# First-layer blocks taken four at a time, with two 64-row remainders side by side in the array

## The chip, the cores and the metric

The kernel runs on one core of one Trainium2 chip, in one launch. The metric is the device time of the whole launch in microseconds; of the kernel before there are three runs, of which the median counts. A profiled execution of its own gives the durations of single instructions.

## What is computed

The input x (8 x 3584 x 192) goes through a causal depthwise filter of 7 taps, whose weights are a softmax per head of 24 channels. The result, 28672 tokens of 192 channels, goes through a layer of 8 experts with a capacity of 3584 tokens each:

```python
out = einsum('hk,bskhg->bshg', softmax(weight), x_unfolded)     # 28672 x 192
logits = out @ w_gate                                           # 28672 x 8
# (token, expert) pairs in falling order of logit; a token goes to the first expert with room
for e in range(8):
    h = maximum(x[assigned == e] @ w1[e], 0)                    # 192 -> 1024
    y[assigned == e] = h @ w2[e]                                # 1024 -> 192
```

All is in 32-bit floats. The kernel splits each factor of the two products into a high part of type float32r and a low part (the rest), and adds three of the four partial products.

## The kernel before, in words

Up to about 164 us of the profile the filter runs as matmuls with a Toeplitz matrix (tile `cv`), with the logits (`pl`) between them; the assignment of tokens to experts is worked out in small steps among all that follows. From then on the class `FFN` works through 56 tiles of 512 tokens of one expert each. What follows is about this second part, and above all about its last 18 tiles (three each of the experts 2 to 7), which start at about 900 us.

`run` (L1455) is a hand-written order. Its outer loop goes over the tiles i, its inner loop over eight stages f. A stage issues, in this order:

- `l1` (L1330): block f of the first layer of tile i, that is 128 of the 1024 hidden rows for 512 tokens. It is five matmuls of 512 columns into one PSUM bank `ph` (pool of 3): (ah, xh), (al, xh), (ah, xl), (dh, xd), (dl, xd). Here ah and al are the high and low parts of the first 128 rows of w1, dh and dl those of the other 64; xa holds the first 128 channels of the tokens, high in xa[:, 0] and low in xa[:, 1]. The array has 128 rows, the remainder 64: xd holds the high part in its rows 0 to 63 and the low part in rows 64 to 127, dh stands twice, and dl (tile `dl`, `DL`) has zeros in rows 64 to 127, which `wpool` puts there once (L1186). Then ScalarE writes hh, the relu of the bank, and VectorE writes hl, the relu less hh.
- `prep` (L1441): a step of the preparation of tile i + 1. In the last tiles that is `shuffle` (L1384): steps 0 to 4 are 16 transposes of 32 x 32 blocks on VectorE (4, 3, 3, 3, 3) from the gathered rows `xg` into `xs`; in step 5 ScalarE writes the high parts xa[:, 0] and xd[0:64]; in step 6 VectorE writes the low parts xa[:, 1] and xd[64:128].
- `l2` (L1349): a quarter of a 128-token block's second layer, for the tile before: four pairs of matmuls (384 and 192 columns) into a bank `y` (pool of 2), with hh and hl of tile i - 1 as the stationary factor. After each odd stage `store` takes the block out: ScalarE writes `yt`, VectorE adds it into `yo`, and GpSimd later scatters `yo` to the output.
- `wsplit` (L1239): weights of a later tile. For the last 18 tiles all parts of w1 were kept in DRAM earlier, and a piece "W1" loads them with two DMAs on SyncE's queue (L1255, L1256), three tiles ahead of their use.

Each engine works through its own instructions in the order of issue. The queue of TensorE holds what `l1` and `l2` issue and, once the assignment is done, nothing else; so in the last 18 tiles the order above is all that sets what stands behind what.

Every matmul, activation and vector instruction of this part is issued through a helper and so has line L56 in the profile; the tile names tell them apart.

Of the kernel before, what the change touches and what calls it, by code (L numbers as in the profile page):

```python
# [6 lines left out]
F32 = mybir.dt.float32  # L7
BF = mybir.dt.bfloat16
I32 = mybir.dt.int32
FR = mybir.dt.float32r  # L10
AF = mybir.ActivationFunctionType
OP = mybir.AluOpType
# [1148 lines left out]
class FFN:  # L1161
# [3 lines left out]
    def __init__(self, tc, nc, attn, w1, w2, out, ident, wr, drm):  # L1165
        self.tc, self.nc = tc, nc

        self.kept1 = [drm.tile([128, 3, F], F32, name="kw%d" % e) for e in range(NE)]
        self.keptd = [drm.tile([64, F], F32, name="kd%d" % e) for e in range(NE)]
        self.scr = [drm.tile([6, 32, 4, 128], F32, name="scr%d" % j) for j in range(2)]  # L1170
        self.kept2 = [drm.tile([128, 8, 2 * D], F32, name="kv%d" % e) for e in range(NE)]
        self.attn, self.w1, self.w2, self.out, self.ident, self.wr = attn, w1, w2, out, ident, wr
        self.bg = lambda: None
        self.busy = lambda: False
        self.WT, self.RAW, self.XG, self.XT, self.H, self.Y, self.XS = {}, {}, {}, {}, {}, {}, {}
        self.wpa, self.wpb, self.DL = [None, None], [None, None], [None, None]
        self.scat, self.late = [], []
        self.free = set()
        self.xg = None


# [57 lines left out]
    def wsplit(self, i, eng):  # L1239

        self.turns += 1
        while self.owed and self.owed[0] <= self.turns:
            self.owed.pop(0)
            self.wload()
        if self.done == len(self.pieces) or self.pieces[self.done][0] > i:
            return
        V, A = self.nc.vector, self.nc.scalar
        _, ky, j, what, q, keep = self.pieces[self.done]
        wp = self.wpa[j]
        e = ky[0]  # L1250
        if what == "W1" or (what, q) == ("a", 0):
            W = wp.tile([128, 3, F], FR, name="w1")
            self.WT[ky] = [W[:, 0], W[:, 1], W[:, 2], self.DL[j]]
        if what == "W1":
            self.nc.sync.dma_start(W.bitcast(F32), self.kept1[e])  # L1255
            self.nc.sync.dma_start(self.DL[j][0:64].bitcast(F32), self.keptd[e])  # L1256
            self.done += 1
            return
        if what == "W2":
            t = self.wpb[j].tile([128, 8, 2 * D], FR, name="w2")  # L1260
            self.WT[ky].append(t)
            self.nc.sync.dma_start(t.bitcast(F32), self.kept2[e])
            self.done += 1
            return
        r = self.RAW.pop(self.done)
        if (what, q) == ("w", 0):
            self.WT[ky].append(self.wpb[j].tile([128, 8, 2 * D], FR, name="w2"))
        t = self.WT[ky]
        if what == "w":
            r = r[:, 0:2 * D].rearrange("p (k d) -> p k d", d=D)  # L1270
            s = slice(2 * q, 2 * q + 2)
            hi, lo = t[4][:, s, 0:D], t[4][:, s, D:2 * D]
        else:
            s = slice(512 * q, 512 * q + 512)
            hi, lo = (t[0][:, s], t[1][:, s]) if what == "a" else (t[2][:, s], t[3][0:64, s])
        A.activation(hi, r, AF.Copy)
        n = 64 if what == "d" else 128
        eng.tensor_tensor(lo, r[0:n], hi[0:n].bitcast(F32), op=OP.subtract)
        S = self.nc.sync
        if not keep:  # L1280
            pass
        elif what == "w":
            S.dma_start(self.kept2[e][:, s], t[4][:, s].bitcast(F32))
        elif what == "a":
            S.dma_start(self.kept1[e][:, 0, s], hi.bitcast(F32))
            S.dma_start(self.kept1[e][:, 1, s], lo.bitcast(F32))
        else:
            S.dma_start(self.kept1[e][:, 2, s], hi.bitcast(F32))
            S.dma_start(self.keptd[e][:, s], lo.bitcast(F32))
        self.done += 1  # L1290
        if ky[1] < NE:
            self.wload()
        else:
            self.owed.append(self.turns + 1)
# [35 lines left out]
    def l1(self, i, key, f):  # L1330
# [15 lines left out]
        nc.dve = max(nc.dve, nc.act)  # L1346
        nc.vector.scalar_tensor_tensor(hl[:, f], p, 0.0, hh[:, f].bitcast(F32), op0=OP.max, op1=OP.subtract)

    def l2(self, i, key, b, half):  # L1349
        nc = self.nc  # L1350
        hh, hl = self.H[i]
        w = self.wt(key)[4]
        if half == 0:
            self.Y[i, b] = self.py.tile([128, 512], F32, name="y")
        y = self.Y[i, b]
        s = slice(128 * b, 128 * b + 128)
        for k in range(4 * half, 4 * half + 4):
            nc.tensor.matmul(y[:, 0:2 * D], hh[:, k, s], w[:, k], start=(k == 0), stop=False, skip_group_check=True)
            nc.tensor.matmul(y[:, 0:D], hl[:, k, s], w[:, k, 0:D], start=False, stop=(k == 7), skip_group_check=True)
            if k % 4 == 1:  # L1360
                self.bg()
# [22 lines left out]
    def shuffle(self, i, step):  # L1384

        V, A = self.nc.vector, self.nc.scalar
        if step == 0:
            self.XS[i] = self.xp.tile([128, 2, 4, 128], F32, name="xs")
            self.XT[i] = (self.xs.tile([128, 2, 512], FR, name="xa"), self.xs.tile([128, 512], FR, name="xd"))
            self.todo = [(q, c) for q in range(4) for c in range(4)]  # L1390
        t = self.XS[i]
        xa, xd = self.XT[i]
        if step < 5:
            for q, c in self.todo[:4 if step == 0 else 3]:

                n = 2 if c < 2 else 1
                s = slice(32 * q, 32 * q + 32)
                x = self.XG[i][s]
                src = x[:, :, 32 * c:32 * c + 32][:, None] if n == 1 else bass.AP(
                    tensor=x.tensor, offset=x.offset + 32 * c, ap=[x.ap[0], [128, 2], [D, 4], [1, 32]])  # L1400
                V.transpose(t[32 * c:32 * c + 32, 0:n, :, s], src)
            del self.todo[:4 if step == 0 else 3]
        a, d = t[:, 0].rearrange("p b t -> p (b t)"), t[0:64, 1].rearrange("p b t -> p (b t)")
        if step == 5:
            self.XG.pop(i)
            A.activation(xa[:, 0], a, AF.Copy)
            A.activation(xd[0:64], d, AF.Copy)
        elif step == 6:
            V.tensor_tensor(xa[:, 1], a, xa[:, 0].bitcast(F32), op=OP.subtract)
            V.tensor_tensor(xd[64:128], d, xd[0:64].bitcast(F32), op=OP.subtract)  # L1410
            self.XS.pop(i)
# [43 lines left out]
    def run(self, idx_of, at, eng, free):  # L1455


        tiles = self.tiles
        n = len(tiles)
        for i in range(n + 1):  # L1460
            at(i)
            for f in range(8):
                if i + 2 < n and f == (4 if tiles[i + 2][1][1] == 4 and tiles[i + 1][1][1] < 4 else 0):
                    self.gather(i + 2, idx_of(tiles[i + 2], True), NTOK if tiles[i + 2][1][1] else NTOK // 2)
                if i < n:
                    self.l1(i, tiles[i][0], f)
                self.bg()
                if i + 2 < n and f == 6 and free() and not self.swapped(i + 2):
                    self.free.add(i + 2)
                if i + 1 < n:  # L1470
                    self.prep(i + 1, f)
                if i + 2 < n and f == 6 and self.swapped(i + 2):
                    self.turn(i + 2, -1)
                if i:
                    self.l2(i - 1, tiles[i - 1][0], f // 2, f % 2)
                    if f % 2:
                        self.store(i - 1, f // 2, idx_of(tiles[i - 1])[f // 2])
                        if f == 7:
                            self.H.pop(i - 1)
                self.bg()  # L1480
                if i < n:
                    self.wsplit(i, eng(f))
                if not f % 2 or i == n and f == 7:
                    self.scatter()
# [9 lines left out]
def moe_kernel(ctx, tc, x, weight, wg, w1, w2, out):  # L1494
    nc = Pace(tc.nc)
# [5 lines left out]
    with ExitStack() as cw:  # L1501
# [4 lines left out]
        oh = pool(cw, "ohp", 5)  # L1506
# [3 lines left out]
        r = Route(tc, nc, LT, lst, wk, drm)  # L1510
        r.oh_pool = oh
        r.bg = lambda: bgp.tile([128, 512], F32, name="bg")
        ff = FFN(tc, nc, attn, w1, w2, out, r.ident, wr, drm)
# [11 lines left out]
        tiles, n = [], 0  # L1525
# [42 lines left out]
        bg = Steps(nc, r, (half(0), tail(), half(1), rest()))  # L1568
# [150 lines left out]
                bg.drain(2)  # L1719

        ff.free = set()
        ff.run(idx_of, at, lambda f: V, lambda: not bg.gens)
    bi = lst.tile([128, 1], I32, name="bi")
    nc.vector.tensor_copy(bi, r.bad)
# [32 lines left out]
```

## Time and profile before

| | |
|---|---|
| three runs: lowest, median, highest | 1235.33, 1237.59, 1238.16 us |
| profiled execution: time, span of its instructions | 1247.95 us, 1246.2 us |
| mean granted TensorE clock | 0.993 |
| TensorE busy | 1208.1 us, 97% |
| VectorE busy | 983.6 us, 79% |
| ScalarE busy | 560.8 us, 45% |
| GpSimd busy | 535.4 us, 43% |

In rows of the profile, PE is TensorE, PEld its loads of stationary factors, DVE VectorE, ACT ScalarE, POOL GpSimd, SPq SyncE's queue. A row "A us, B" of the timeline gives the start in us from the span's start and the length; instructions of one kind in a row are put together with their count, and idle time of the engine ahead of them stands in brackets with what ended it. Matmuls are pipelined: a matmul's length includes its way through the array, so that two in a row overlap, and what one costs is the distance from its start to the next one's.

### The profile page before, as it was taken

How to read it: one execution, taken by the hardware profiler on the slowest of the kernel's cores; microseconds unless marked ns; L12 is line 12 of the kernel's file. 1: busy time of each engine (PE TensorE's matmuls, PEld its weight loads, DVE VectorE, ACT ScalarE, POOL GpSimd, SP SyncE). 2: the span in 40 equal slices, each digit the busy share in tenths (PEclk: the TensorE clock that was granted, in tenths of full speed). 3: DMA queues.
4: the chain of work that ended last, by engine and by line, in shares of the span. 5: the costliest groups of instructions: out<-in, count | busy, mean ns of one | idle time of the engine just before them, and what ended most of it. 6: DMA issues, size and time to landing. Idle time of an engine off the chain costs nothing.

```text
span 1246.2 us, 21782 instructions
## 1 busy us (share of the span) xinstructions
PE 1208.1 (97%) x7694; PEld 1036.6 (83%) x7694; DVE 983.6 (79%) x2122; ACT 560.8 (45%) x1251; POOL 535.4 (43%) x524
## 2 busy tenths in 40 slices
PE   5999899999999999999999999999999999999997
PEld 2445578889989898889888889999999999999997
DVE  7388778988898988889889866777777777777772
ACT  4454455556435554445544443333333333343332
POOL 3000233535455554555465445445434544444522
PEclk9999999999999999999999999999999999999999
DMA  9999664569526473746343442114233222413100
GB/s 242 332 338 321 216 220 123 147 156 305 170 85 176 156 229 110 246 132 216 102 132 98 128 106 73 38 46 158 72 118 107 96 98 96 158 58 136 48 23 28
DMA packets 129220, 182.02 MB, mean 146 GB/s; under 512 B 21632, under 2 KB 91728, under 8 KB 127440
## 3 DMA queue, kind: packets, MB, share of 16 engines
q1 hardware_dynamic: 86496, 104.15, 27.5%
q0 software_dynamic: 21504, 44.07, 11.9%
q10 hardware_dynamic: 21104, 32.34, 7.9%
q8 instruction: 62, 1.02, 0.3%
q14 instruction: 54, 0.44, 0.1%
HBM read 102.38 MB, written 78.12 MB: 145 GB/s over the span
## 4 chain that ended last, share of the span: by engine, by line
PE 83%; DVE 6%; DMA 5%; issue 2%; ACT 1%; SPq 1%; another core or an unknown queue 0%; POOL 0%; POOLq 0%; ACTq 0%; DVEq 0%
PE ph L56 39%; PE y L56 38%; DMA X<-in_x_dram 4%; PE cv L56 2%; PE bg L56 2%; DVE X L56 1%; DVE aT L56 1%; DMA attn<-a 1%; DVE hl L56 1%; PE pl L56 1%; DMA raw<-in_moe_w_dram 1%; PE px L56 0%; DVE yo L56 0%; SPq L569 0%
## 5 line engine op out<-in xcount | busy, mean ns | idle before, releaser
L56 PE MATMUL y<-w,hh 128*128 128x384 f32 x1792 | 535.6, 355 | 0.0
L56 ACT ACTIVATE hh<-ph 128x512 fp32r<-128x512 f32 x448 | 267.7, 598 | 451.1 <-PE ph L56 389.6
L56 PE MATMUL y<-w,hl 128*128 128x192 f32 x1792 | 448.9, 251 | 0.0
L56 DVE SCALAR_TENSOR_TENSOR hl<-ph,hh 128x512 fp32r<-128x512 f32 x448 | 307.8, 687 | 128.7 <-ACT hh L56 101.4
L56 PE MATMUL ph<-xa,w 128*128 128x512 f32 x1344 | 395.2, 402 | 0.2 <-DVE hl L56 0.2
L56 PEld LDWEIGHTS y<-w,hl 128*128 128x128 f32 x1792 | 340.9, 190 | 16.2
L56 PEld LDWEIGHTS y<-w,hh 128*128 128x128 f32 x1792 | 336.3, 188 | 20.9 <-issue 2.9
L1377 POOL DMA_INDIRECT out_dram<-yo,ia x128 | 145.3, 1135 | 236.8 <-DVE yo L56 194.0
L56 PEld LDWEIGHTS ph<-xa,w 128*128 128x128 f32 x1344 | 218.4, 189 | 21.4 <-issue 1.6
L1377 POOL DMA_INDIRECT out_dram<-yo,ib x96 | 95.2, 991 | 220.5 <-DVE yo L56 213.1
L56 PE MATMUL ph<-xd,w 128*128 128x512 f32 x448 | 177.4, 396 | 0.0
L1302 POOL DMA_INDIRECT xg<-attn,ja x128 | 141.3, 1104 | 80.8 <-issue 39.2
L56 PE MATMUL ph<-xd,dl 128*128 128x512 f32 x448 | 174.2, 389 | 0.2 <-issue 0.2
L56 DVE STREAM_TRANSPOSE xs<-xg 32x128 f32<-32x128 f32 (+2 forms) x408 | 164.8, 404 | 6.6
L56 ACT ACTIVATE yt<-y 128x192 f32<-128x192 f32 x224 | 73.1, 326 | 111.5 <-PE y L56 71.8
L56 PE MATMUL cv<-X,TH 118*128 118x384 f32 x256 | 104.5, 536 | 17.7 <-DVE TH L56 11.4
L56 DVE TENSOR_TENSOR yo<-y,yt 128x192 f32<-128x192 f32 x224 | 79.2, 354 | 49.6 <-ACT yt L56 46.0
L1302 POOL DMA_INDIRECT xg<-attn,jb x96 | 103.6, 1079 | 29.3 <-issue 29.3
L56 PEld LDWEIGHTS ph<-xd,dl 128*128 128x128 f32 x448 | 84.2, 188 | 20.2 <-issue 0.5
L56 PEld LDWEIGHTS ph<-xd,w 128*128 128x128 f32 x448 | 84.0, 187 | 19.7 <-issue 0.6
L56 PEld LDWEIGHTS cv<-X,TH 118*128 118x128 f32 x256 | 46.7, 203 | 50.0 <-issue 15.0
L56 ACT ACTIVATE a<-cv 128x384 f32<-128x384 f32 x128 | 59.7, 492 | 50.0 <-PE cv L56 26.9
(237 smaller groups left out, 920.2 us busy)
## 6 DMA issues: line engine op xcount, KB each, us to landing
attn<-a ACTq DMA_DIRECT2D x16, 1344.0 KB
X<-in_x_dram SPq DMA_DIRECT2D x17, 672.0 KB
raw<-in_moe_w_dram SPq DMA_DIRECT2D x56, 192.0 KB
X<-in_x_dram ACTq DMA_DIRECT2D x15, 672.0 KB
kw<-w SPq DMA_DIRECT2D x36, 256.0 KB
kv<-w SPq DMA_DIRECT2D x24, 384.0 KB
scr<-xs SPq DMA_DIRECT2D x96, 96.0 KB
w<-kw SPq DMA_DIRECT2D x6, 1536.0 KB
```

The costliest lines, as they stand in the source:

```text
L56: return f(*a, **k)
L1302: self.nc.gpsimd.indirect_dma_start(out=t[:, b], out_offset=None, in_=self.attn[0:rows], in_offset=bass.IndirectOffsetOnAxis(ap=idx[b], ax ...
L1377: st = self.nc.gpsimd.indirect_dma_start(out=self.out, out_offset=bass.IndirectOffsetOnAxis(ap=idx, axis=0), in_=o, in_offset=None, bounds ...
```

## The change

It concerns the tiles whose w1 was loaded by a "W1" piece, the last 18. Three things are different there.

First, `l1x4` takes the place of `l1`. In stages 0 and 4 it does four blocks at once; in the other stages of such a tile there is no first-layer work. Of its four banks one is of the pool `bg` (2 banks, idle by then), three are the `ph` banks. It issues the first four matmuls of each of the four blocks, then the four matmuls with dl, then the four pairs of hh and hl. `prep`, `l2`, `store` and the rest stay at their stages.

Second, the four matmuls with dl have 64 rows each. Those of even blocks use rows 0 to 63 of `dl` and of xd, those of odd blocks rows 64 to 127 of `dl` and of a new tile xe, so that neighbours stand in different halves of the array's rows and write to different banks.

Third, for this dl is loaded from DRAM twice, into both halves, and step 5 of `shuffle` writes the high part of the 64 channels a second time on ScalarE, into xe[64:128] (a buffer named `oa`).

```diff
+        self.both = set()
+        self.XE = {}
...
-            self.nc.sync.dma_start(self.DL[j][0:64].bitcast(F32), self.keptd[e])
+            for q in range(2):
+                self.nc.sync.dma_start(self.DL[j][64 * q:64 * q + 64].bitcast(F32), self.keptd[e])
+            self.both.add(ky)
...
+    def l1x4(self, i, key, f0):
+
+        nc = self.nc
+        if f0 == 0:
+            self.H[i] = (self.hp[i % 2].tile([128, 8, 512], FR, name="hh"),
+                         self.hp[i % 2].tile([128, 8, 512], FR, name="hl"))
+        hh, hl = self.H[i]
+        ah, al, dh, dl = self.wt(key)[0:4]
+        xa, xd = self.XT[i]
+        xe = self.XE[i]
+        ps = [self.more("bg") if f == f0 else self.ph.tile([128, 512], F32, name="ph") for f in range(f0, f0 + 4)]
+        for f, p in zip(range(f0, f0 + 4), ps):
+            s = slice(128 * f, 128 * f + 128)
+            for n, (wt, xx) in enumerate(((ah, xa[:, 0]), (al, xa[:, 0]), (ah, xa[:, 1]), (dh, xd))):
+                nc.tensor.matmul(p, wt[:, s], xx, start=(n == 0), stop=False)
+        for f, p in zip(range(f0, f0 + 4), ps):
+            s, r = slice(128 * f, 128 * f + 128), slice(64 * (f % 2), 64 * (f % 2) + 64)
+            nc.tensor.matmul(p, dl[r, s], (xe if f % 2 else xd)[r], start=False, stop=True)
+        for f, p in zip(range(f0, f0 + 4), ps):
+            nc.scalar.activation(hh[:, f], p, AF.Relu)
+            nc.dve = max(nc.dve, nc.act)
+            nc.vector.scalar_tensor_tensor(hl[:, f], p, 0.0, hh[:, f].bitcast(F32), op0=OP.max, op1=OP.subtract)
...
             A.activation(xd[0:64], d, AF.Copy)
+            if self.tiles[i][0] in self.both:
+                self.XE[i] = self.more("xe")
+                A.activation(self.XE[i][64:128], d, AF.Copy)
...
-                if i < n:
+                if i in self.XE:
+                    if f % 4 == 0:
+                        self.l1x4(i, tiles[i][0], f)
+                elif i < n:
                     self.l1(i, tiles[i][0], f)
...
+        ff.more = lambda name: r.bg() if name == 'bg' else oh.tile([128, 512], FR, name='oa')
```

What this moves is seen best in the second half of a tile, stages 4 to 7. On VectorE, before, from the hl of stage 4 to the end of the tile (`xs<-xg` are transposes of step 4, `xa<-xs,xa` and `xd<-xs,xd` the low parts of step 6):

```order
L56 SCALAR_TENSOR_TENSOR hl<-ph,hh 128x512
L56 STREAM_TRANSPOSE xs<-xg 32x8x32
L56 STREAM_TRANSPOSE xs<-xg 32x4x32 x2
L56 SCALAR_TENSOR_TENSOR hl<-ph,hh 128x512
L56 TENSOR_TENSOR yo<-y,yt 128x192
L56 SCALAR_TENSOR_TENSOR hl<-ph,hh 128x512
L56 TENSOR_TENSOR xa<-xs,xa 128x512
L56 TENSOR_TENSOR xd<-xs,xd 64x512
L56 SCALAR_TENSOR_TENSOR hl<-ph,hh 128x512
L56 TENSOR_TENSOR yo<-y,yt 128x192
```

And now, on VectorE at the same place, up to the first hl of the next tile:

```order
L56 SCALAR_TENSOR_TENSOR hl<-bg,hh 128x512
L56 SCALAR_TENSOR_TENSOR hl<-ph,hh 128x512 x3
L56 STREAM_TRANSPOSE xs<-xg 32x8x32
L56 STREAM_TRANSPOSE xs<-xg 32x4x32 x2
L56 TENSOR_TENSOR yo<-y,yt 128x192
L56 TENSOR_TENSOR xa<-xs,xa 128x512
L56 TENSOR_TENSOR xd<-xs,xd 64x512
L56 TENSOR_TENSOR yo<-y,yt 128x192
L56 SCALAR_TENSOR_TENSOR hl<-bg,hh 128x512
```

All four hl stand ahead of the transposes of step 4 and of both low parts, where one and three stood before. On ScalarE, before, from the hh of stages 4 and 5 on (`xa<-xs` and `xd<-xs` are the high parts of step 5):

```order
L56 ACTIVATE hh<-ph 128x512 x2
L56 ACTIVATE xa<-xs 128x512
L56 ACTIVATE xd<-xs 64x512
L56 ACTIVATE yt<-y 128x192
L56 ACTIVATE hh<-ph 128x512 x2
```

And now, on ScalarE at the same place:

```order
L56 ACTIVATE hh<-bg 128x512
L56 ACTIVATE hh<-ph 128x512 x3
L56 ACTIVATE xa<-xs 128x512
L56 ACTIVATE xd<-xs 64x512
L56 ACTIVATE oa<-xs 64x512
L56 ACTIVATE yt<-y 128x192 x2
```

The high parts stand behind four hh instead of two, the copy into xe (`oa`) behind them, and both yt of the second half behind that.

## The prediction

> **What bounds the kernel now.** I read the page first: the busy times, then the chain of work that ended last.
>
> ```profile
> PE 1208.1 (97%) x7694; PEld 1036.6 (83%) x7694; DVE 983.6 (79%) x2122; ACT 560.8 (45%) x1251; POOL 535.4 (43%) x524
> PE 83%; DVE 6%; DMA 5%; issue 2%; ACT 1%; SPq 1%; another core or an unknown queue 0%; POOL 0%; POOLq 0%; ACTq 0%; DVEq 0%
> ```
>
> TensorE is the bound of the whole. The change touches only the last 18 tiles, so I asked for busy times by stage there; the other rows are stretches around two changes of the clock, used further down.
>
> ```profile
> core 0: us, PE busy (x) PEld busy (x) DVE busy (x) ACT busy (x) POOL busy (x), PEclk, DMA share, GB/s
> 907.00:1235.70 328.70, 328.70 (x1879) 298.94 (x1879) 241.81 (x514) 123.78 (x248) 138.22 (x134) 1.00 0.25 87
> ...
> 24.00:27.40 3.40, 1.26 (x4) 0.38 (x2) 2.27 (x3) 1.47 (x3) 0.00 (x0) 1.00 1.09 303
> 27.40:34.20 6.80, 5.96 (x24) 2.94 (x24) 1.98 (x3) 1.31 (x3) 0.00 (x0) 0.50 1.06 371
> 41.10:44.50 3.40, 1.76 (x20) 0.76 (x18) 2.11 (x3) 0.20 (x1) 0.00 (x0) 1.00 1.06 349
> 146.90:150.30 3.40, 1.05 (x10) 0.30 (x2) 0.57 (x1) 0.00 (x0) 2.79 (x4) 1.00 0.31 84
> 150.30:157.10 6.80, 5.81 (x39) 3.41 (x43) 4.69 (x6) 2.45 (x7) 4.55 (x5) 0.50 0.26 72
> ```
>
> In the first of these rows TensorE is busy 328.70 of 328.70 us: in these tiles it waits for nothing, and each first-layer matmul taken away would be worth its full distance, as long as nothing else becomes late. VectorE has 241.81 / 328.70 = 74% of the stretch: it keeps up, but only because its work comes in eight even portions. The timeline around the end of one tile (stages 6 and 7, then the next tile) shows both, TensorE and VectorE together:
>
> ```profile
> 1060.11 0.88 PE L56 MATMUL ph<-xa,w 128*128 128x512 f32 x3
> ...
> 1060.83 0.40 PE L56 MATMUL ph<-xd,w 128*128 128x512 f32 x1
> 1061.06 0.39 PE L56 MATMUL ph<-xd,dl 128*128 128x512 f32 x1
> 1061.08 0.36 DVE L56 TENSOR_TENSOR yo<-y,yt 128x192 f32<-128x192 f32 x1 [0.56 <-ACT yt L56]
> 1061.29 0.34 PE L56 MATMUL y<-w,hh 128*128 128x384 f32 x1
> ...
> 1061.48 0.60 ACT L56 ACTIVATE hh<-ph 128x512 fp32r<-128x512 f32 x1 [0.44 <-PE ph L56]
> ...
> 1062.12 0.69 DVE L56 SCALAR_TENSOR_TENSOR hl<-ph,hh 128x512 fp32r<-128x512 f32 x1 [0.68 <-ACT hh L56]
> ...
> 1062.40 0.88 PE L56 MATMUL ph<-xa,w 128*128 128x512 f32 x3
> 1062.72 0.68 DVE L56 TENSOR_TENSOR xa<-xs,xa 128x512 fp32r<-128x512 f32 x1
> ...
> 1063.44 0.69 DVE L56 TENSOR_TENSOR xd<-xs,xd 64x512 fp32r<-64x512 f32 x1
> ```
>
> A stage is 1062.40 - 1060.11 = 2.29 us: 1.18 us of first layer (to 1061.29) and 1.11 us of second. A dl matmul costs 1061.29 - 1061.06 = 0.23 us. The low parts of the next tile are written by 1063.44 + 0.69 = 1064.13; that tile begins one stage after 1062.40, at 1064.69, and reads xd in its fourth matmul, 0.72 us later. The margin is 1.3 us, and it rests on VectorE getting to the low parts right after the hl of stage 6.
>
> **The dl matmuls.** 18 tiles have 144 of them; 36 groups hold two pairs each. Whether neighbours run side by side in the two row halves, the trace doesn't show. It shows the like for column strips: `pl` matmuls stand in four strips of 32 columns. The row of 48, four transposes that use the whole array, and the way into strips and out again:
>
> ```profile
> 142.54 1.52 PE L56 MATMUL pl<-aT,c_mu 128*32 128x128 f32 x48
> ```
>
> ```profile
> 159.13 0.60 PE L56 MATMUL bg<-ident,xg 128*128 128x128 f32 x4
> ```
>
> ```profile
> 169.64 0.64 PE L56 MATMUL bg<-aT,c_mu 128*32 128x128 f32 x16
> 170.22 0.50 PE L56 MATMUL ph<-xd,w 128*128 128x512 f32 x1
> 170.55 0.40 PE L56 MATMUL ph<-xd,dl 128*128 128x512 f32 x1
> 170.88 0.65 PE L56 MATMUL bg<-aT,c_mu 128*32 128x128 f32 x16
> ```
>
> One such matmul is some 0.27 us long, so 48 start within 1.25 us, 0.027 us apart, against (0.60 - 0.27) / 3 = 0.11 us for whole-array ones of the same width: four side by side at full effect. I take two row halves to do the same, 0.24 us a pair. But the passage costs: from the dl matmul at 170.55 to the strips at 170.88 it is 0.33 us instead of 0.23, so 0.1 us is lost on the way in. The 16 strips have their last start near 169.64 + 0.64 - 0.27 = 170.01, and the next matmul starts 0.21 us later, where a round of four takes 0.11: 0.1 us lost on the way out. The matmul behind that is again 0.33 us away from its neighbour (170.22 to 170.55), another 0.1 us, as its stationary factor wasn't loaded ahead. Strips of 32 columns load quickly; a 128-column dl should lose that last 0.1 us on the way in too. So a group goes from 4 x 0.23 = 0.92 us to 2 x 0.24 + 4 x 0.1 = 0.88 us: a gain of 0.04 us, for 36 groups 1.4 us. The ends: if the passage costs nothing, 0.92 - 0.46 per group, 17 us gained; if the halves don't run side by side, 0.92 + 0.40 per group, 14 us lost. I stay in between, at the row of the passage, since that is a measured change of the array's division in this kernel.
>
> The Trainium skill speaks against the change at this place: TensorEngine Tiling (Array Packing), Key Properties, says that changing the mode drains the array, which the 0.1 us on either side agree with; its Theoretical Speedup (up to 2x where the contraction is 64 or less) taken alone would give the 17 us of gain.
>
> **The regrouping, which decides.** The preparation of the next tile stays at its stages, but in the second half of a tile it now stands behind four hl instead of being spread between them. I count from S, the start of the first dl matmul of the second group. For ScalarE's and VectorE's distances two more views, each engine's own timeline:
>
> ```profile
> 1060.21 0.62 ACT L56 ACTIVATE xd<-xs 64x512 fp32r<-64x512 f32 x1
> 1060.73 0.31 ACT L56 ACTIVATE yt<-y 128x192 f32<-128x192 f32 x1
> ```
>
> ```profile
> 1057.08 0.36 DVE L56 TENSOR_TENSOR yo<-y,yt 128x192 f32<-128x192 f32 x1
> 1057.54 0.69 DVE L56 SCALAR_TENSOR_TENSOR hl<-ph,hh 128x512 fp32r<-128x512 f32 x1
> 1058.26 1.08 DVE L56 STREAM_TRANSPOSE xs<-xg 32x256 f32<-32x256 f32 x3
> ```
>
> - hh of the first bank starts 0.42 us after its dl matmul (1061.06 to 1061.48); ScalarE's 512-element copies follow each other at 0.52 us (1060.21 to 1060.73), so it never holds VectorE up.
> - hl of the first bank starts 0.64 us after its hh, at S + 1.06. hl to the next instruction is 0.60 us (1062.12 to 1062.72) to 0.72 us (1057.54 to 1058.26); with 0.62 the fourth starts at S + 2.92.
> - The three transposes of step 4: 0.72 us later, 1.08 us long, done at S + 4.72.
> - ScalarE: xa high at S + 4.76, xd high at 5.28, the new xe at 5.80, then yt of stage 5 at 6.32. VectorE may not pass the yo of stage 5, which waits for that yt: 0.35 us later (1060.73 to 1061.08), S + 6.67.
> - xa low 0.4 us later (0.36 to 0.46), S + 7.07; xd low 0.72 us after that (1062.72 to 1063.44), S + 7.79, done at S + 8.48. The fourth matmul of the next tile can start at S + 8.52.
> - TensorE meanwhile: second pair, passage out and first load, S + 0.68; four second-layer quarters of 1.11 us, S + 5.12; its next tile's fourth matmul would be due 0.72 us on, at S + 5.84.
>
> TensorE, in order, stands still for 8.52 - 5.84 = 2.68 us, with all the rest of that tile behind it. Nothing covers this: the second layer of the tile before has been used up. It happens at the 17 borders between two of the 18 tiles (the first was prepared in the old order): 17 x 2.68 = 45.6 us. Ends: the handovers may be 0.15 us shorter or 0.4 us longer in all; with side-by-side pairs at no cost TensorE is ready 0.22 us sooner and waits as much longer, and with no overlap 0.48 us less.
>
> The first half of a tile just fits. The page's group of the transposes:
>
> ```profile
> L56 DVE STREAM_TRANSPOSE xs<-xg 32x128 f32<-32x128 f32 (+2 forms) x408 | 164.8, 404 | 6.6
> ```
>
> After four hl VectorE has 13 of them and two yo: 2.92 + 0.72 + 13 x 0.404 + 2 x 0.46 = 9.8 us after the first group's first dl, and its next hl is due at 10.2 us (a half-tile of 4 x 2.29 - 0.04 = 9.1 us and 1.06). The banks are free in time (`bg` alternates, and the last hl of a group is over 3 us before the next group's second block), and so are the `y` banks. xe adds a ScalarE copy of 0.62 us (0.52 of distance), which is in the chain above. The second load of dl is 256 KB on SyncE's queue, behind a load of six times that and three tiles ahead of use, at a DMA share of 0.25: nothing, and without that cover a few us at six places.
>
> **Sum.** 45.6 - 1.4 = 44 us more. The profiled execution took 1247.95 us (a span of 1246.2 and 1.75 around it) and would take 1292; it lies 10.4 us above the median of the three runs, 1237.59, whose sum is 1281.6.
>
> **The rivals.**
> - *The halves don't run side by side.* Against it: the strips' 0.027 us. For it: no row splits the rows. Lost 14 us in the groups, the wait is 17 x (2.68 - 0.48) = 37 us: +51, 1289.
> - *The clock halves.* In the rows above, a stretch of 3.40 us with 1.26 or 1.05 us busy (37% and 31%) is followed by 6.8 us at a clock of 0.50; one with 1.76 (52%) is not. The new wait leaves TensorE idle for about 1.7 us ahead of the third matmul and 0.3 us ahead of the fourth, so that a stretch of 3.4 us that holds all of it is about 38% busy, on the edge. 6.8 us at half clock cost 3.4 us. If one tile in three is hit, 6 x 3.4 = 20 us on top: 1302; if all are, 58 us: 1339. The Trainium skill, TensorE: Matmul & The Clock Gate, in its closing table, asks for no idle gap above about 3 us, and by that no tile would be hit; the rows here show halving after stretches that were not empty.
> - *A shorter wait*, if the handovers or VectorE's order are kinder by about half of it: +22, 1260.
> - *The other side, faster:* no wait at all. The four second-layer quarters, 4.44 us, would have to cover the chain to the low parts; that decides at S + 5.84, 2.7 us before what I get. With pairs at no cost it would give -17, 1221; with the passage as above -1.4, no change. It is also the case in which the regrouping doesn't do what the order of instructions says.
>
> **Chances and range.** Forecast 0.58, no overlap 0.15, half clock 0.16, shorter wait 0.04, no wait 0.07 (faster 0.05, no change 0.02). The three runs span 0.23% of their median, so I call 0.2% (2.5 us) the least that can be told from no change. The forecast's own ends are +26 (pairs at no cost, short handovers) and +58 (no overlap, long ones), 1264 to 1296; with a third of the tiles at half clock taken in, I give 1264 to 1304. Left out are half clock everywhere, the shorter wait and no wait, with about 0.17. Faster 0.05, same 0.02, slower 0.93.
>
> **What the profile after would show.** Idle time of TensorE ahead of `bg<-xa` at each border of the last tiles, released by VectorE's `xa`, and a shorter one by its `xd`; tile to tile some 20.8 us instead of 8 x 2.29 = 18.3; hl in fours; and dl matmuls that start in pairs with almost no distance, about 0.33 us behind a 128-row one. I am wrong if TensorE stays without gaps there, if the granted clock drops in the last 18 tiles, or if the dl matmuls start 0.23 us apart.

## The result, and the profile after

The changed kernel takes 1294.02 us (median of four runs, 1293.30 to 1294.66) against 1236.46 us for the one before in the same runs: 57.6 us more, a ratio of 1.0467 with a 95% interval of 1.0452 to 1.0482. The time lies in the predicted range and on the predicted side, 12.4 us above the number.

The page of the profiled execution, busy times and the chain that ended last:

```profile
PE 1224.4 (95%) x7694; PEld 1024.7 (79%) x7694; DVE 973.5 (75%) x2122; ACT 565.9 (44%) x1269; POOL 533.5 (41%) x524
PE 79%; DVE 9%; DMA 4%; ACT 3%; issue 3%; SPq 1%; POOL 0%; POOLq 0%; ACTq 0%; DVEq 0%
```

TensorE's share of the span falls from 97% to 95%, and VectorE's share of the chain rises from 6% to 9%. The waits of TensorE in the last 18 tiles (us in total, times, longest):

```profile
PE bg L56 <- DVE xa L56: 30.3, 17, 1.8
PE bg L56 <- DVE xd L56: 5.2, 17, 0.3
```

Before, there were none there. There are 17 of each, one at every border between two of the 18 tiles, as long each time. The list counts idle time only from a matmul's recorded end on, and that lies behind the point where the next one could start (a lone matmul is 0.49 us long in the rows below, against a distance of 0.23 us between starts); so its 35.5 us in sum are less than what the borders cost, which is worked out further down. One border in the timeline, all engines (second-layer matmuls left out):

```profile
1055.06 0.49 PE L56 MATMUL bg<-xd,dl 64*128 64x512 f32 x1
1055.07 0.49 PE L56 MATMUL ph<-oa,dl 64*128 64x512 f32 x1
1055.40 0.39 PE L56 MATMUL ph<-xd,dl 64*128 64x512 f32 x1
1055.40 0.39 PE L56 MATMUL ph<-oa,dl 64*128 64x512 f32 x1
1055.59 0.60 ACT L56 ACTIVATE hh<-bg 128x512 fp32r<-128x512 f32 x1 [3.75 <-PE ph L56]
1056.09 1.57 ACT L56 ACTIVATE hh<-ph 128x512 fp32r<-128x512 f32 x3
1056.22 0.69 DVE L56 SCALAR_TENSOR_TENSOR hl<-bg,hh 128x512 fp32r<-128x512 f32 x1 [0.93 <-ACT hh L56]
1056.83 1.87 DVE L56 SCALAR_TENSOR_TENSOR hl<-ph,hh 128x512 fp32r<-128x512 f32 x3
1058.72 1.08 DVE L56 STREAM_TRANSPOSE xs<-xg 32x256 f32<-32x256 f32 x3
1059.83 0.63 ACT L56 ACTIVATE xa<-xs 128x512 fp32r<-128x512 f32 x1 [2.17 <-DVE xs L56]
1060.37 0.61 ACT L56 ACTIVATE xd<-xs 64x512 fp32r<-64x512 f32 x1
1060.52 0.73 PE L56 MATMUL bg<-xa,w 128*128 128x512 f32 x2
1061.01 0.63 ACT L56 ACTIVATE oa<-xs 64x512 fp32r<-64x512 f32 x1
1061.66 0.55 ACT L56 ACTIVATE yt<-y 128x192 f32<-128x192 f32 x2
1062.02 0.36 DVE L56 TENSOR_TENSOR yo<-y,yt 128x192 f32<-128x192 f32 x1 [2.23 <-ACT yt L56]
1062.30 0.68 DVE L56 TENSOR_TENSOR xa<-xs,xa 128x512 fp32r<-128x512 f32 x1
1063.01 0.69 DVE L56 TENSOR_TENSOR xd<-xs,xd 64x512 fp32r<-64x512 f32 x1
1063.03 0.49 PE L56 MATMUL bg<-xa,w 128*128 128x512 f32 x1 [1.79 <-DVE xa L56]
...
1063.84 0.47 PE L56 MATMUL bg<-xd,w 128*128 128x512 f32 x1 [0.32 <-DVE xd L56]
```

Read it from the top: the dl matmuls start two at a time; hh and hl run in fours; the transposes come after all four hl; VectorE then stands idle for 2.23 us, waiting for a yt that ScalarE may only write after the three copies of step 5; the low parts come last of all. TensorE has begun the next tile at 1060.52, does the two matmuls that need high parts alone, and stands still. The two dl matmuls of a pair are side by side.

Two more rows of each kernel show how far apart the tiles are (the low part of xd, once per tile), first after, then before:

```profile
1063.01 0.69 DVE L56 TENSOR_TENSOR xd<-xs,xd 64x512 fp32r<-64x512 f32 x1
1084.06 0.69 DVE L56 TENSOR_TENSOR xd<-xs,xd 64x512 fp32r<-64x512 f32 x1
```

```profile
1063.44 0.69 DVE L56 TENSOR_TENSOR xd<-xs,xd 64x512 fp32r<-64x512 f32 x1
1081.73 0.69 DVE L56 TENSOR_TENSOR xd<-xs,xd 64x512 fp32r<-64x512 f32 x1
```

From tile to tile it is 21.05 to 21.08 us instead of 18.29. But every third time it is 22.6 us. There the clock is halved, which the sums by stretch show (the column before the DMA share is the granted clock; the first two rows are a stretch and the one right behind it, and so are the last two; no half clock follows the row between them):

```profile
908.87:912.28 3.41, 1.32 (x5) 0.74 (x5) 2.00 (x4) 1.15 (x3) 1.49 (x2) 1.00 0.80 274
912.28:915.69 3.41, 3.41 (x10) 2.64 (x9) 0.00 (x0) 0.00 (x0) 2.73 (x3) 0.50 0.74 273
...
953.24:956.66 3.42, 1.82 (x7) 1.32 (x8) 2.00 (x4) 0.47 (x2) 2.20 (x2) 1.00 0.45 123
973.73:977.14 3.41, 1.32 (x5) 0.86 (x5) 2.00 (x4) 1.02 (x3) 1.61 (x2) 1.00 0.87 299
977.14:980.55 3.41, 3.41 (x9) 2.65 (x8) 0.00 (x0) 0.00 (x0) 2.62 (x3) 0.50 0.67 249
```

Six such halvings lie in the last 18 tiles, at 912.3 us and then every 64.8 us. Each follows a stretch that holds the whole wait or all but 0.3 us of it, and lasts 3.41 us. So the 57.6 us come apart: 17 x (21.07 - 18.29) = 47.3 us at the borders and 6 x (22.6 - 21.07) = 9.2 us for the clock, 56.5 in sum.

The span grows by only 46.3 us (1292.5 against 1246.2), because the execution of before that was profiled had lost some 10 us ahead of the part in question: its first low part of these tiles is written at 898.80 us, that of the changed kernel at 888.97 us. From there to the end of the span it is 403.6 us against 347.4, 56.2 us more, which agrees with the sum above.

### The profile page after: what moved, and what is told of

Its sections match the earlier page's. It is cut to its first block, busy times and chain, and to the rows that moved or that the text cites. A ratio compares the mean times of both kernels' runs of the same rounds, so it can differ in the third digit from the quotient of the medians.

```text
span 1292.5 us, 21824 instructions
## 1 busy us (share of the span) xinstructions
PE 1224.4 (95%) x7694; PEld 1024.7 (79%) x7694; DVE 973.5 (75%) x2122; ACT 565.9 (44%) x1269; POOL 533.5 (41%) x524
## 4 chain that ended last, share of the span: by engine, by line
PE 79%; DVE 9%; DMA 4%; ACT 3%; issue 3%; SPq 1%; POOL 0%; POOLq 0%; ACTq 0%; DVEq 0%
PE ph L56 36%; PE y L56 33%; PE bg L56 6%; DVE hl L56 3%; PE cv L56 3%; DMA X<-in_x_dram 1%; DVE xs L56 1%; DVE aT L56 1%; PE pl L56 1%; DMA wgr<-in_moe_w_gate_dram 1%; DVE X L56 1%; DMA attn<-a 1%; DVE xd L56 1%; DVE xa L56 1%; ACT hh L56 1%
## 5 line engine op out<-in xcount | busy, mean ns | idle before, releaser
L56 PE MATMUL ph<-xa,w 128*128 128x512 f32 x1236 | 367.8, 406 | 0.0
L56 ACT ACTIVATE hh<-ph 128x512 fp32r<-128x512 f32 x412 | 238.3, 600 | 294.2 <-PE ph L56 290.5
L56 DVE SCALAR_TENSOR_TENSOR hl<-ph,hh 128x512 fp32r<-128x512 f32 x412 | 275.8, 684 | 67.4 <-ACT hh L56 63.8
L56 PEld LDWEIGHTS ph<-xa,w 128*128 128x128 f32 x1236 | 214.1, 193 | 29.6 <-issue 1.8
L56 PE MATMUL ph<-xd,w 128*128 128x512 f32 x412 | 165.6, 402 | 0.0
L56 PE MATMUL ph<-xd,dl 128*128 128x512 f32 (+1 forms) x340 | 132.4, 390 | 0.2 <-DVE dl L56 0.2
L1306 POOL DMA_INDIRECT xg<-attn,jb x96 | 99.6, 1038 | 29.3 <-issue 29.0
L56 DVE SCALAR_TENSOR_TENSOR hl<-bg,hh 128x512 fp32r<-128x512 f32 x36 | 24.9, 692 | 102.1 <-ACT hh L56 102.1
L56 ACT ACTIVATE hh<-bg 128x512 fp32r<-128x512 f32 x36 | 21.6, 600 | 171.0 <-PE ph L56 171.0
L56 PEld LDWEIGHTS ph<-xd,w 128*128 128x128 f32 x412 | 79.0, 192 | 18.4 <-issue 0.4
```

What stands on the lines that cost most here:

```text
L56: return f(*a, **k)
L1306: self.nc.gpsimd.indirect_dma_start(out=t[:, b], out_offset=None, in_=self.attn[0:rows], in_offset=bass.IndirectOffsetOnAxis(ap=idx[b], ax ...
```

## Experiments

The theory: TensorE waits at the borders because the next tile's low parts stand behind four hl and, through the yo of stage 5, behind the three copies of step 5; the clock halves as a consequence; the row halves themselves cost and gain next to nothing. The rivals: the row halves cost (drains, loads, banks); the slower every third tile comes from its weights being loaded, not from the clock. Two sets of runs were made, on two chips. On the second the kernel before takes 1247.45 us instead of 1234.48, so each run is compared with the kernel before of its own set. That difference arises ahead of the last 18 tiles: their first low part is written at 885 to 888 us in the profiles of the first set and at 896 to 900 us in those of the second.

**The regrouping without the halves.** Groups of four, but four 128-row dl matmuls in each, dl loaded once, no xe:

```diff
-            s, r = slice(128 * f, 128 * f + 128), slice(64 * (f % 2), 64 * (f % 2) + 64)
-            nc.tensor.matmul(p, dl[r, s], (xe if f % 2 else xd)[r], start=False, stop=True)
+            s = slice(128 * f, 128 * f + 128)
+            nc.tensor.matmul(p, dl[:, s], xd, start=False, stop=True)
```

> The regrouping alone: groups of four banks as in the changed kernel, but the four dl matmuls of a group use all 128 rows (dl with zeros below, no second load of dl, no xe). If the regrouping is what costs (the low parts of the next tile stand behind four hl), the time stays far above before: per border the chain is some 0.1 us shorter at its start and 0.65 us shorter without xe ahead of yt, and TensorE is ready 0.4 us later because there is no pair side by side, so about 1.85 us of wait are left at 17 borders, +31 us, and the waits are too short for the clock to halve: 1267 us (1260 to 1276). If the row halves are what costs (drains, loads, banks), it falls back to the time before, 1236 to 1240 us.

Measured: 1264.44 us, ratio 1.0250 (1.0234 to 1.0265), 30.0 us more than before, inside the 1260 to 1276 us expected. No clock below 1 in the last tiles, and the waits are shorter (TensorE's, in total):

```profile
PE bg L56 <- DVE xa L56: 16.8, 17, 1.0
PE bg L56 <- DVE xd L56: 5.3, 17, 0.3
```

About half of the loss (30.0 of 57.6 us) is there with no row half in the kernel, so the rival falls for this part. Borders are 20.05 us apart here. Of what the changed kernel has on top, 9.2 us are the clock and 17 x (21.07 - 20.28) = 13.4 us the copy into xe, by the run below that moves it. The other 0.23 us per border (20.28 against 20.05), 3.9 us in all, go with the halves: before the second group's first dl matmul there are 0.32 us instead of 0.23, and from it to its hh 0.53 instead of 0.43.

**The low parts ahead of the yo.** The changed kernel with step 6 issued in stage 5, right behind step 5:

```diff
-                    self.prep(i + 1, f)
+                    for step in ((5, 6) if f == 5 else () if f == 6 else (f,)) if i in self.XE else (f,):
+                        self.prep(i + 1, step)
```

> The changed kernel with one step moved: in the last tiles step 6 (the low parts of xa and xd) is issued in stage 5 right behind step 5, so it stands ahead of the yo of stages 5 and 7 and no longer waits for a yt that stands behind xe. By the wait theory xd low ends 1.8 us sooner at 17 borders, -30 us, and the remaining wait of about 1 us is too short for the clock to halve, -9 us: 1255 us (1248 to 1264). If the wait is set by the four hl alone, or the halves cost, it stays above 1280 us.

Measured: 1250.77 us, ratio 1.0136 (1.0120 to 1.0151): 16.3 us more than before. The 1255 us expected are 20.5 above the 1234.48 of this set. Only the shorter of the two waits is left in the list:

```profile
PE bg L56 <- DVE xd L56: 3.7, 17, 0.2
```

Tile to tile is 19.21 us, so having the yo in front of the low parts cost 21.07 - 19.21 = 1.86 us per border; 1.8 were expected. TensorE's first matmul of a tile is held by xa high as well, here and in the changed kernel, but by less than 0.1 us.

**The copy into xe out of the chain.** The changed kernel with that copy moved from step 5 to stage 7:

```diff
-            if self.tiles[i][0] in self.both:
-                self.XE[i] = self.more("xe")
-                A.activation(self.XE[i][64:128], d, AF.Copy)
...
+        elif step == 7:
+            self.XS.pop(i)
+            if self.tiles[i][0] in self.both:
+                self.XE[i] = self.more("xe")
+                A.activation(self.XE[i][64:128], d, AF.Copy)
```

> The changed kernel with one copy moved: ScalarE's copy into xe is issued in stage 7, behind the yt of stage 5, instead of ahead of it. The chain to the low parts then lacks one copy of 0.65 us at 17 borders, -11 us, and the wait left (about 1.4 us) is too short for the clock to halve, -9 us: 1274 us (1268 to 1280). If VectorE's low parts don't hang on that yt, the time stays at 1294 us.

Measured: 1282.95 us beside 1247.45 for the one before, ratio 1.0289 (1.0261 to 1.0316). The expected number was given for the other set; as a difference it is 35.5 us over before instead of 57.6, so 22 us less than the changed kernel, where 20 were expected. Borders are 20.28 us apart. The clock was expected not to halve at all; it does so once in these tiles instead of six times, behind the first of these two stretches:

```profile
1160.38:1163.80 3.42, 2.12 (x10) 1.20 (x10) 2.00 (x4) 2.20 (x5) 1.21 (x2) 0.99 0.50 151
1163.80:1167.20 3.40, 3.40 (x10) 2.67 (x9) 0.00 (x0) 0.00 (x0) 2.79 (x3) 0.51 0.91 370
```

**Four idle matmuls inside the wait.** They write a bank that is never read:

```diff
+                if f == 0 and n == 2:
+                    px = self.pt.tile([128, 512], F32, name="px")
+                    for _ in range(4):
+                        nc.tensor.matmul(px, ah[:, s], xa[:, 0], start=True, stop=True)
                 nc.tensor.matmul(p, wt[:, s], xx, start=(n == 0), stop=False)
```

> The changed kernel with four idle matmuls (into a bank that is never read) between the second and the third matmul of each of the last 18 tiles, where TensorE waits 1.8 us anyway. They add 4 x 0.23 us of activity inside the wait and should take no time of their own. If the six slower borders among the 17 (22.6 us from border to border instead of 21.1) come from the clock that halves after a stretch with too little activity, they go: -9 us, 1285 us (1282 to 1288), and no row of the clock below 1 in the last tiles. If they come from the weights that are loaded every third tile, they stay: 1294 us; if the matmuls do take time, 17 x 0.9 = 15 us more.

Measured: 1284.47 us, ratio 1.0407 (1.0391 to 1.0423), 50.0 us over before: 7.6 us less than the changed kernel's 57.6, with more work. The same stretch of both kernels, first the changed one, then this one:

```profile
897.20:1259.00 361.80, 326.24 (x1739) 267.96 (x1739) 227.14 (x507) 118.94 (x251) 131.14 (x128) 0.97 0.25 81
```

```profile
897.20:1259.00 361.80, 341.92 (x1856) 281.92 (x1855) 228.99 (x509) 121.54 (x256) 133.72 (x130) 1.00 0.24 81
```

The mean clock is 1.00 instead of 0.97, and all borders are 21.05 to 21.09 us apart; the slow third ones are gone although their weights are loaded as before. So it was the clock, and it was the lack of activity that halved it. (The four matmuls are not wholly free: from the start of these tiles to the end the gain is 8.4 us, where the six slow borders were worth 9.2.)

**The preparation ahead of the second group.** Halves, groups, xe and the double load as in the change; all transposes in stages 0 to 3, steps 5 and 6 at the head of stage 4:

```diff
+                if i in self.XE and f == 4 and i + 1 < n:
+                    self.prep(i + 1, 5)
+                    self.prep(i + 1, 6)
                 if i in self.XE:
                     if f % 4 == 0:
...
-                    self.prep(i + 1, f)
+                    for step in ((0,), (1,), (2, 3), (4,), (), (), (), ())[f] if i in self.XE else (f,):
+                        self.prep(i + 1, step)
```

> The changed kernel with the next tile's preparation moved wholly ahead of the second group: all 16 transposes in stages 0 to 3, steps 5 and 6 at the start of stage 4 ahead of the group's hh and hl. Groups, halves, xe and the second load of dl stay. By the wait theory TensorE never stands still at a border: about 1.4 us less than before, 1235 us (1231 to 1241). If the row halves, the passages or the extra load cost beyond what they were put at, it stays above by that much: 14 us if a passage costs 0.4 us more per group, 1250 us.

Measured: 1233.73 us against 1234.48, ratio 0.9994 (0.9985 to 1.0003). All of the loss is gone by the order of the preparation alone, ScalarE's three copies included; the halves, the groups, xe and the second load of dl are all still there. TensorE has no idle time in the last tiles:

```profile
907.00:1220.00 313.00, 313.00 (x1786) 269.64 (x1785) 222.19 (x496) 119.99 (x253) 130.14 (x130) 1.00 0.28 93
```

With no wait left it is also the fair measure of what the change was about: next to nothing.

**The same without the halves.** Early preparation, full rows:

> The early preparation with full rows: as the run with the preparation ahead of the second group, but without the row halves (four 128-row dl matmuls per group, dl loaded once, no xe). What is left of the difference to that run is the net worth of the 72 pairs after their passages. By the term of the prediction the pairs gain 0.04 us per group, so this one is 1.4 us slower than the run with halves: 1235 us against 1233.7. In the profile the borders of that run lie 18.28 us apart against 18.29 before, which would make the two equal within 0.5 us. If the halves gained their full 17 us and something else took it back, this would be 1240 us or more.

Measured: ratio 0.9989 (0.9976 to 1.0002), not to be told from the run with the halves; that it would be 1.4 us slower did not come true. The distance of tiles says it more sharply: 18.25 us here against 18.28 us with halves, both without waits. So the pairs of a tile cost 0.03 us instead of gaining; the 0.04 us that this kernel gains on 18.29 come with the grouping.

**Twice the passages.** Early preparation, groups of two blocks:

```diff
-        ps = [self.more("bg") if f == f0 else self.ph.tile([128, 512], F32, name="ph") for f in range(f0, f0 + 4)]
+        ps = [self.more("bg") if f == f0 else self.ph.tile([128, 512], F32, name="ph") for f in range(f0, f0 + 2)]
...
-                    if f % 4 == 0:
+                    if f % 2 == 0:
                         self.l1x4(i, tiles[i][0], f)
```

> The price of a passage: early preparation as before, but groups of two blocks (72 groups with one pair each, so twice as many passages for the same pairs). By four times 0.1 us per passage a group of two goes from 2 x 0.23 = 0.46 to 0.24 + 0.4 = 0.64 us or a little more: 72 x 0.18 to 0.22 us = 13 to 16 us over the time before, 1248 to 1250 us, with no waits. If passages are free, it equals the groups of four, 1234 us.

Measured: 1257.97 us against 1247.45, ratio 1.0098 (1.0069 to 1.0127): 10.5 us more by the medians, 12 by the ratio, a little under the 13 to 16 expected. TensorE waits for nothing in these tiles. Tile to tile is 18.96 us, 0.71 us over the run with full rows, for four groups: 0.18 us each. A pair saves one matmul of 0.23 us, so the passage there and back costs 0.41 us. In the timeline of this kernel:

```profile
1051.00 0.39 PE L56 MATMUL ph<-xd,w 128*128 128x512 f32 x1
1051.32 0.49 PE L56 MATMUL bg<-xd,dl 64*128 64x512 f32 x1
1051.32 0.50 PE L56 MATMUL ph<-oa,dl 64*128 64x512 f32 x1
1051.75 0.44 PE L56 MATMUL y<-w,hh 128*128 128x384 f32 x1
1052.03 0.25 PE L56 MATMUL y<-w,hl 128*128 128x192 f32 x1
```

It is 0.32 us on the way in instead of 0.23, then 0.43 us for one pair, and 0.28 us from the first second-layer matmul to the next, where it is 0.17 us before (1061.29 to 1061.46).

**Fewer passages.** Groups of six banks (px joins), one per tile; blocks 6 and 7 keep full rows, against xe with zeros in its rows 0 to 63. The preparation is spread differently: ten transposes a tile earlier, the rest and the low parts ahead of stage 6.

```diff
+        ps = [self.more("bg") if f < 2 else self.pt.tile([128, 512], F32, name="px") if f == 2 else
+              self.ph.tile([128, 512], F32, name="ph") for f in range(6)]
...
+                self.nc.gpsimd.memset(self.XE[i][0:64].bitcast(F32), 0.0)
...
-                    self.prep(i + 1, f)
+                    for step in () if i in self.XE else (f,):
+                        self.prep(i + 1, step)
...
+                if i in self.XE:
+                    if f == 1:
+                        self.out4(i, self.rest, 4, 6)
+                    if i + 1 < n:
+                        for step in {3: (3, 4), 5: (5, 6)}.get(f, ()):
+                            self.prep(i + 1, step)
+                if f == 7 and i + 2 < n and i + 1 in self.XE:
+                    for step in (0, 1, 2):
+                        self.prep(i + 2, step)
```

(`out4` writes hh and hl of some of the group's banks; those of the fifth and sixth follow after the first `store`.)

> Fewer passages: groups of six banks (the bank px, idle by then, joins two bg and three ph), one per tile with three pairs; the other two blocks keep 128-row dl matmuls, against xe with zeros in its upper half. Ten of the 16 transposes of a tile are moved a tile earlier, the rest and the low parts stand ahead of the seventh block's hl. One passage of 0.43 us for three pairs: 6 x 0.23 = 1.38 us becomes 0.72 + 0.43 = 1.15, 18 x 0.23 = 4 us less than before: 1230.5 us, ratio 0.997. If TensorE waits anywhere again (the banks of six hl, or the low parts), it is above 1236 us.

Measured: 1243.58 us against 1247.45, ratio 0.9971 (0.9959 to 0.9983): 3.6 us faster than before, where 4 were expected, and the only version whose interval lies below 1. Tile to tile is 17.93 to 17.98 us, which over 18 tiles would be 6 us; 1.3 us of them are lost at the end of the kernel, where 8.9 us follow the last matmul instead of 7.6. Three pairs behind one passage, in its timeline:

```profile
1067.91 0.49 PE L56 MATMUL bg<-xd,dl 64*128 64x512 f32 x1
1067.91 0.49 PE L56 MATMUL bg<-oa,dl 64*128 64x512 f32 x1
1068.24 0.39 PE L56 MATMUL px<-xd,dl 64*128 64x512 f32 x1
1068.25 0.39 PE L56 MATMUL ph<-oa,dl 64*128 64x512 f32 x1
1068.48 0.39 PE L56 MATMUL ph<-xd,dl 64*128 64x512 f32 x1
1068.48 0.39 PE L56 MATMUL ph<-oa,dl 64*128 64x512 f32 x1
1068.80 0.44 PE L56 MATMUL y<-w,hh 128*128 128x384 f32 x1
```

The first pair takes 0.33 us to the next start, the second 0.24, the last 0.32: between two others a pair takes the time of one matmul, and the first and the last carry the passage. How much of the 0.3 us per tile against the run with full rows is due to the pairs and how much to the larger group was not tested apart.

## Why the prediction was right, and where not

- **TensorE waits for nothing before, and only for VectorE's low parts after.** Right: 17 borders, released by xa and then by xd.
- **The chain from S.** Right, link by link: counted from the first dl matmul at 1055.06, the first hl starts at +1.16 (predicted 1.06), the transposes at +3.66 (3.64), xa high at +4.77 (4.76), yt at +6.60 (6.32), xa low at +7.24 (7.07), xd low at +7.95 (7.79), the fourth matmul at +8.78 (8.52). The dl matmul's own exposed load was left out at the start, and two ScalarE copies out of `xs` are 0.65 us apart around xe rather than 0.52. Against a kernel with the same groups and no wait (18.28 us per tile) the wait is 2.79 us; predicted 2.68. Sum 47.4 us; predicted 45.6. That it came so close is partly luck: the fourth matmul was 0.26 us later than predicted (8.78 against 8.52), and so was TensorE. In the run with the early preparation, where nothing holds it up, it begins the next tile at S + 5.38 instead of 5.12, as four second-layer quarters in a row take 4.72 us there and not four times the 1.11 us of the kernel before.
- **The pairs.** Right that they run side by side and that the passage eats it up: predicted a gain of 0.04 us per group, measured -0.015 (18.28 against 18.25 us, two groups per tile). The rival without overlap falls, as the two of a pair start within 0.01 us of each other.
- **The half clock.** This is the step that failed: the forecast put it at nothing, and a drop of the clock in the last 18 tiles was one of the signs of being wrong that the prediction names. It stood among the rivals with a chance of 0.16, at one tile in three and 3.4 us each. That 57.6 us still lie within the forecast's own ends (+26 to +58) is luck: the upper end was meant for pairs that do not overlap and longer handovers, not for the clock. It came, at one tile in three, for 1.53 us each: it lasted 3.41 us instead of the 6.8 us of the rows before, and such a stretch can cost at most half of itself, 1.7 us. Those 9.2 us, 1.8 us of the wait and 1.2 us that the pairs did not gain make up nearly all of the difference (57.6 us measured, 44 predicted). The rows of before had put the case on the edge (about 38% busy predicted, 1.32 of 3.41 us, 39%, measured at the first). What was missing is how the wait falls on a grid of 3.41 us. That it was one tile in three fits such a grid: two tiles of 21.07 us and one of 22.6 are 64.7 us, and 19 stretches are 64.85, so that every third wait falls on nearly the same place of the grid. This explanation was not tested by itself.
- **Faster, no change, or a shorter wait.** Fell with the wait as measured; the run with the early preparation shows what no wait would have taken.

## What to carry to other kernels

When work of one engine is put together in larger groups, write down anew what its consumers' engines have queued behind each group: here the sum of VectorE's work did not grow, yet the new order cost 47 us at the borders, 13 of them by one more copy on ScalarE, and moving five of VectorE's instructions per tile (three transposes and the two low parts) and ScalarE's three copies ahead of the group gave all of it back. Splitting the array for a few matmuls is paid per passage, here 0.4 us there and back against 0.23 us saved per pair, so two pairs come out even and it starts to pay at the third. A wait that recurs once per tile should be checked against what it does to the clock, not only added up.

## What the runs showed of the hardware

Two 64-row matmuls in the two row halves start within 0.01 us of each other (1055.06 and 1055.07 us), and so do the loads of their stationary factors (both at 1055.06). Between a 128-row matmul and such a pair, about 0.1 us is lost in each direction: 0.32 us instead of 0.23 on the way in, 0.32 instead of 0.24 on the way out. Another 0.1 us goes in each direction behind the first matmul (0.33 us instead of 0.24, and 0.28 instead of 0.17), whose load starts together with it instead of ahead of it (1055.06 on the way in, 1055.72 on the way out).

The clock halves after stretches on a fixed grid of 3.41 us that were far from idle. The grid shows in the changed kernel's halvings: from those at 31.64 and 48.71 us to that at 912.28 us and the next at 977.14 us it is 17.07, 863.57 and 64.85 us, which are 5, 253 and 19 times 3.413 us. The busy time of the profile is no clean measure for it, as it holds the pipeline's tail and waits for loads: 1.32 us of 3.41 busy was followed by half clock, 1.82 was not, but in the run with the late xe copy a stretch with 2.12 was. Counted instead by the columns streamed (0.227 us for 512, the distance in dense rows), an estimate, the stretches of the last 18 tiles that were followed by half clock had 0.24 to 0.40 of their length filled (the changed kernel and the one with the late xe copy), and those that were not had 0.38 or more; so the border for these matmuls is near 0.4. This holds for the matmuls of these tiles alone; no run here shows it for others. The Trainium skill, TensorE: Matmul & The Clock Gate, puts it in its closing table at gaps above about 3 us; in the last tiles of the changed kernel no gap was longer than 1.8 us, and the clock halved six times, so here the trace does not agree.
